# Scaling half of the query features by a ratio of softmax sums, in a four-layer kernel on one Trainium2 core

## The chip, the cores and the metric

The kernel runs on one core of a Trainium2 chip. The metric is the device time of one execution in microseconds (us); lower is better. A core has a matrix engine (PE, with weight loads listed apart as PEld), a vector engine (DVE), an activation engine (ACT), a general engine (POOL), and SP, which here only issues DMAs. Each engine works through its own stream of instructions in order, and they wait for one another through semaphores.

## The reference, cut to what matters

Two kinds of layer alternate: A, B, A, B. Each adds its result to `x` after a layer norm. Layer A goes through 64 segments of 32 tokens; the memory of a segment comes out of the segment before, so A is a chain. Layer B is linear attention; its features are softmaxes over the 20 features of a head:

```python
pq = einsum('bhsd,hdf->bhsf', q, w_phi);  pk = the same of k
phi_q = concatenate([softmax(pq), softmax(-pq)], axis=-1)
phi_k = concatenate([softmax(pk), softmax(-pk)], axis=-1)
kv = einsum('bhsf,bhsd->bhfd', phi_k, v)
z  = sum over s of phi_k
o  = einsum('bhqf,bhfd->bhqd', phi_q, kv) / (einsum('bhqf,bhf->bhq', phi_q, z) + 1e-06)
```

There are 2048 tokens, width 640, 32 heads of 20 features, two halves (called `sg` 0 and 1 in the kernel). A factor that is common to both halves of `phi_q` of one token and head appears above and below the line of the last quotient.

## The kernel before

**Layer A.** `A_pre` first computes what doesn't depend on the chain. `A_chain` then runs the 64 segments. One segment is, on PE, twelve projections of 20 matmuls with 32 weight columns each (`project`, L943, results `ps_qk` and `ps_v`), scores (`ps_s`), sums, attention (`ps_o`), four rounds of 48 output matmuls (`wo_round`, L1019, `ps_w`), and 14 matmuls into a spare bank (`keep_busy`, L1026, `ps_idle`). Its order is written out by hand. The weights of a segment stream in from HBM all the time, issued by SP. In the first segment of a chain `fill(FILL[li])` puts weight loads of one column each into PE's stream after the first projection; every segment has `SEG_FILL` = 1 more. They compute nothing.

**Layer B.** `layer_B` works on four groups of 512 tokens. Heads are packed six to a chunk of 120 partitions (`CH`), six chunks (`NC_`), the last of two heads; a feature array `phi` has a half, a chunk and a token index. In each group `keys_values` does keys and values; `queries` (L447) multiplies out the query features and ACT writes `exp(pq)` and `exp(-pq)` into both halves of `phi` (L450); `query_norms`, one group later, makes them softmaxes:
- 12 matmuls with the 0/1 matrix `osum` add up the features of each head and half in one bank, `ps_sq` (L457);
- `reciprocal_rows` makes the reciprocals as `exp(-log(sum))` on ACT, Ln L346, Exp L348 (bf16) and Exp L349 (fp32), and a DVE subtraction L350 leaves in the upper 64 partitions the remainder that bf16 lost;
- 12 matmuls with the 0/1 matrix `expd` spread the reciprocals over the features (`ps_e`, L464), and DVE multiplies each chunk of each half in place (L465).

After the last group `kvm` and `zm` are taken from PSUM (L511, L514). The tail then does, for each group, `denominators` (12 matmuls into `ps_den`, L522, and `reciprocal_rows` again), `attention` (L533, L536, L538, L539) and `output_rows` (L550, L552, and in the first B layer the next layer norm, whose centring is L244 on POOL). `query_norms` of the last group stands after `attention(0)`. `late_constants` builds `osum`, `zm` and `expd` during group 1 on POOL (L318, L324, L326, L329). `side_bank` is a pool of two PSUM banks that `ps_sq`, `ps_e` and `ps_den` share. Inside layer B the order of each engine's instructions is set by a planner, with the program's order as its input; the A layers are outside it.

Of the kernel before, what the change touches and what calls it, by code (L numbers as in the profile page):

```python
# [17 lines left out]
SLOTS = {"Q": 3, "K": 3, "V": 3}  # L18
LN_EPS = 1e-5

FILL = {0: 86, 2: 78}
SEG_FILL = 1

LATE = 64512
# [3 lines left out]
def ap3(ap, dims):  # L28
    return bass.AP(tensor=ap.tensor, offset=ap.offset, ap=[list(d) for d in dims])
# [86 lines left out]
class Kernel:  # L116
# [133 lines left out]
    def layer_B(self, x_dram, at_dram, xout_dram, xnext_dram, li, bp, post):  # L250


        nc, tc, KC, D = self.nc, self.tc, self.KC, self.Dm
        DH, H = self.DhB, self.HB
        HC = 6
        CH = DH * HC
        NC_ = -(-H // HC)
        sizes = [min(CH, D - CH * c) for c in range(NC_)]
# [5 lines left out]
        def take(nbytes):  # L264
            nonlocal at
            at += nbytes
            return at - nbytes

        f4 = NC_ * 512 * 2
        wo = self.view(take(NC_ * D * 2), NC_ * D * 2).rearrange("p (c m) -> p c m", m=D)  # L270
        osum, zm = [self.view(take(f4 // 2), f4 // 2).rearrange("p (s c m) -> p s c m", s=2, m=P) for _ in range(2)]
        expd = self.view(take(4 * NC_ * CH), 4 * NC_ * CH).rearrange("p (s c d) -> p s c d", s=2, d=DH)
        kvm = self.view(take(4 * NC_ * CH), 4 * NC_ * CH).rearrange("p (s c m) -> p s c m", s=2, m=CH)
        lgs, hls = self.views(take(4096), 2048, 2, F32), self.views(take(2048), 1024, 2)
        oTs = self.views(take(2 * f4), f4, 2)
# [6 lines left out]
        blk = self.view(take(32), 2 * HC)  # L282
# [10 lines left out]
        phi = self.view(ARENA - fb, fb).rearrange("p (s c t) -> p s c t", s=2, c=NC_)  # L293
        with tc.tile_pool(name=f"B{li}_kv", bufs=1, space=bass.MemoryType.PSUM, reuse_waits="tile") as kvp, \
                tc.tile_pool(name=f"B{li}_pt", bufs=2, space=bass.MemoryType.PSUM, reuse_waits="tile") as ptp, \
                tc.tile_pool(name=f"B{li}_ps", bufs=3, space=bass.MemoryType.PSUM, reuse_waits="tile") as pp:
            def bank(name="ps_b", dt=F32):
                return pp.tile([P, 512 if dt == F32 else 1024], dt, name=name, tag="bank")

            def side_bank(name):  # L300
                return ptp.tile([P, 512], F32, name=name, tag="side")

            nc.gpsimd.memset(wbd[:], 0.0)
            for i in range(HC):
# [10 lines left out]
            expc = expd[:, :, :, :].rearrange("p s (c h) d -> p s c (h d)", h=HC)  # L315

            def late_constants():
                nc.gpsimd.memset(osum[:], 0.0)  # L318
                nc.vector.memset(zm[:], 0.0)
                for sg in range(2):  # L320
                    for c in range(NC_):
                        nh = sizes[c] // DH
                        o = osum[:, sg, c, :].rearrange("p (u h) -> p u h", u=2)[:, :, 32 * sg + HC * c:32 * sg + HC * c + nh]
                        nc.gpsimd.tensor_copy(out=o, in_=bcast_mid(blk[:, 0:nh], 2))  # L324

                nc.gpsimd.memset(expd[:], 0.0)  # L326
                for sg in range(2):
                    for u in range(2):
                        nc.gpsimd.affine_select(out=expd[:, sg], in_=expd[:, sg], compare_op=ALU.not_equal, fill=1.0,  # L329
                                                base=-(32 * sg + 64 * u), pattern=[[-1, NC_ * HC], [0, DH]],  # L330
                                                channel_multiplier=1)
# [3 lines left out]
            eps6 = bp.tile([P, 1], F32, name="eps6")  # L335
            nc.vector.memset(eps6[:], 1e-6)
            kv_ps = [kvp.tile([P, 512], F32, name=f"kv{j}") for j in range(3)]

            def kv_out(sg, c):
                j = NC_ * sg + c  # L340
                return kv_ps[j // 4][0:sizes[c], 126 * (j % 4):126 * (j % 4) + 21 * (sizes[c] // DH)]

            def reciprocal_rows(ps, bias):

                lg = lgs.next()
                nc.scalar.activation(out=lg[:], in_=ps[:, :], func=ACT.Ln, bias=bias)  # L346
                hl = hls.next()
                nc.scalar.activation(out=hl[:], in_=lg[:], func=ACT.Exp, scale=-1.0)  # L348
                nc.scalar.activation(out=lg[64:P, :], in_=lg[64:P, :], func=ACT.Exp, scale=-1.0)  # L349
                nc.vector.tensor_tensor(out=hl[64:P, :], in0=lg[64:P, :], in1=hl[64:P, :], op=ALU.subtract)  # L350
                return hl

            def load_rows(g):
                for b in range(4 * g, 4 * g + 4):
# [96 lines left out]

            def query_norms(g):
                tk = slice(512 * g, 512 * g + 512)
                ps = side_bank("ps_sq")
                for i in range(2 * NC_):
                    sg, c = i // NC_, i % NC_
                    nc.tensor.matmul(ps[:, :], lhsT=osum[0:sizes[c], sg, c, :], rhs=phi[0:sizes[c], sg, c, tk],  # L457
                                     start=(i == 0), stop=(i == 2 * NC_ - 1))
                hl = reciprocal_rows(ps, 0.0)
                for i in range(2 * NC_):  # L460
                    sg, c = i // NC_, i % NC_
                    mc = sizes[c]
                    pe = side_bank("ps_e")
                    nc.tensor.matmul(pe[0:mc, :], lhsT=expc[:, sg, c, 0:mc], rhs=hl[:, :], start=True, stop=True)  # L464
                    nc.vector.tensor_tensor(out=phi[0:mc, sg, c, tk], in0=phi[0:mc, sg, c, tk], in1=pe[0:mc, :], op=ALU.mult)  # L465


            with tc.issue_after(self.last_load.ins):
# [38 lines left out]
            for sg in range(2):  # L507
                for c in range(NC_):
                    mc, nh = sizes[c], sizes[c] // DH
                    o = kv_out(sg, c).rearrange("p (h f) -> p h f", f=DH + 1)  # L510
                    nc.vector.tensor_tensor(out=kvm[0:mc, sg, c, 0:mc].rearrange("p (h f) -> p h f", f=DH), in0=o[:, :, 0:DH],  # L511
                                            in1=mask[0:mc, 0:nh, :], op=ALU.mult)
                    for u in range(2):
                        nc.vector.tensor_tensor(out=zm[0:mc, sg, c, 64 * u + HC * c:64 * u + HC * c + nh], in0=o[:, :, DH],  # L514
                                                in1=blk[0:mc, 0:nh], op=ALU.mult)

            def denominators(g):
                tk = slice(512 * g, 512 * g + 512)
                ps = side_bank("ps_den")
                for i in range(2 * NC_):  # L520
                    sg, c = i // NC_, i % NC_
                    nc.tensor.matmul(ps[:, :], lhsT=zm[0:sizes[c], sg, c, :], rhs=phi[0:sizes[c], sg, c, tk],  # L522
                                     start=(i == 0), stop=(i == 2 * NC_ - 1))
                return reciprocal_rows(ps, eps6[:])

            def attention(g, hl):
                tk = slice(512 * g, 512 * g + 512)
                oT = oTs.next().rearrange("p (c t) -> p c t", c=NC_)
                for c in range(NC_):
                    mc = sizes[c]  # L530
                    pn = bank("ps_num")
                    for sg in range(2):
                        nc.tensor.matmul(pn[0:mc, :], lhsT=kvm[0:mc, sg, c, 0:mc], rhs=phi[0:mc, sg, c, tk], start=(sg == 0),  # L533
                                         stop=(sg == 1))
                    pe = side_bank("ps_e")
                    nc.tensor.matmul(pe[0:mc, :], lhsT=expc[:, 0, c, 0:mc], rhs=hl[:, :], start=True, stop=True)  # L536
# [335 lines left out]
    def A_chain(self, xn_dram, at_dram, li, load_slot, piece, load_wo, late_wo, wo_mid, wo_end, low):  # L872
# [3 lines left out]
        with tc.tile_pool(name=f"A{li}_ch", reuse_waits="tile", bufs=1) as sp, \  # L876
# [196 lines left out]
            for s in range(NSEG):  # L1073
# [19 lines left out]
                if s == 0:  # L1093
                    fill(FILL[li])
                to_rows(q_or_k("K", 0), "K")
# [141 lines left out]
```

## Time and profile before

| what | value |
|---|---|
| median of 3 runs | 3733.62 us (3727.46 to 3739.32) |
| profiled execution | 3733.58 us, of which 3731.6 us are the span |
| PE, DVE, ACT, POOL busy | 95%, 63%, 55%, 45% of the span |
| first chain, first to last store of a segment | 1345.75 us |
| from there to the first store of the second chain (first B layer, second `A_pre`) | 501.3 us |
| second chain, first to last store | 1405.15 us |
| from there to the end (second B layer) | 272.5 us |

The stages are bounded by the stores of a segment's rows (`attn<-Vp`, 64 in each chain). The shares are averages over stages with different limits, so the table by stage says more than the busy shares of the whole. "Idle before" in a list of groups is the idle time of an engine just before the instructions of that group, and "issue" stands for time in which the engine waited for nothing that the profile names.

### The profile page before, as it was taken

How to read it: one execution, taken by the hardware profiler on the slowest of the kernel's cores; microseconds unless marked ns; L12 is line 12 of the kernel's file. 1: busy time of each engine (PE TensorE's matmuls, PEld its weight loads, DVE VectorE, ACT ScalarE, POOL GpSimd, SP SyncE). 2: the span in 40 equal slices, each digit the busy share in tenths (PEclk: the TensorE clock that was granted, in tenths of full speed). 3: DMA queues.
4: the chain of work that ended last, by engine and by line, in shares of the span. 5: the costliest groups of instructions: out<-in, count | busy, mean ns of one | idle time of the engine just before them, and what ended most of it. 6: DMA issues, size and time to landing. Idle time of an engine off the chain costs nothing.

```text
span 3731.6 us, 168901 instructions
## 1 busy us (share of the span) xinstructions
PE 3537.4 (95%) x71010; PEld 2312.5 (62%) x71318; DVE 2365.5 (63%) x6334; ACT 2038.1 (55%) x5225; POOL 1665.2 (45%) x4325
## 2 busy tenths in 40 slices
PE   9999999999999999989898999999999999999898
PEld 7766666666666666555376666666666666665553
DVE  6566666666666666466633666666666666666475
ACT  3356666666666656455423655556555555555363
POOL 3345555555555555330622444454444444544400
PEclk9999999999999999989899999999999999999999
DMA  9988788887888878812297778777777777877500
GB/s 304 336 296 288 277 286 282 286 293 278 291 280 288 295 267 296 299 59 81 95 290 235 273 265 281 279 264 273 274 272 279 263 270 279 283 272 276 171 1 29
DMA packets 531731, 933.33 MB, mean 250 GB/s; under 512 B 141066, under 2 KB 298394, under 8 KB 530970
## 3 DMA queue, kind: packets, MB, share of 16 engines
q1 hardware_dynamic: 428794, 818.87, 62.3%
q0 software_dynamic: 68512, 90.42, 7.9%
q10 hardware_dynamic: 33664, 13.24, 1.4%
q8 instruction: 557, 9.13, 1.0%
q14 instruction: 204, 1.67, 0.1%
HBM read 852.43 MB, written 73.73 MB: 248 GB/s over the span
## 4 chain that ended last, share of the span: by engine, by line
PE 38%; DVE 6%; ACT 4%; issue 4%; DMA 2%; PEld 2%; POOL 2%; SPq 0%; POOLq 0%; DVEq 0%; ACTq 0%
PE ps_qk L943 10%; PE ps_v L943 5%; PE ps_w L1019 5%; PE ps_o L993 3%; PE ps_s L985 2%; DVE hT L899 2%; PE ps_s L1051 2%; PE ps_pq L447 2%; PE ps_s L980 1%; PEld L834 1%; PE ps_pre L834 1%; PE ps_idle L1026 1%; PE ps_v L426 1%; DVE E L1058 1%; ACT raw L953 1%
## 5 line engine op out<-in xcount | busy, mean ns | idle before, releaser
L943 PEld LDWEIGHTS <-hT 128*32 128x32 bf16 x30720 | 745.0, 96 | 507.0 <-issue 90.4
L943 PE MATMUL ps_qk<-arena,hT 128*32 128x384 bf16 x20480 | 1004.5, 328 | 14.8 <-DMA arena<-in_A_Wq_dram 2.8
L953 ACT ACTIVATE raw<-ps_qk 128x384 bf16<-128x384 f32 x1024 | 503.0, 491 | 382.1 <-PE ps_s L1051 246.3
L943 PE MATMUL ps_v<-arena,hT 128*32 128x384 bf16 x10240 | 569.0, 330 | 43.7 <-issue 36.2
L926 POOL DMA_DIRECT2D Vp<-vb x512 | 259.6, 507 | 716.9 <-PE ps_o L993 473.1
L1019 PE MATMUL ps_w<-arena,OT 128*32 128x160 bf16 x24576 | 533.1, 235 | 15.8 <-DMA arena<-wo_rows 9.5
L1019 PEld LDWEIGHTS <-OT 128*32 128x32 bf16 x24576 | 434.3, 97 | 101.6 <-issue 25.1
L958 DVE STREAM_TRANSPOSE KT<-raw 128x384 bf16<-128x384 bf16 x512 | 296.2, 578 | 197.7 <-ACT raw L953 193.7
L961 DVE STREAM_TRANSPOSE QT<-raw 128x256 bf16<-128x256 bf16 x512 | 228.0, 445 | 238.4 <-ACT raw L953 196.0
L914 POOL DMA_DIRECT2D kqb<-kqb x512 | 292.3, 571 | 174.6 <-POOL KT L922 146.2
L974 DVE CAST Vp<-ps_v 64x384 bf16<-64x384 f32 x512 | 286.2, 559 | 118.7 <-ACT Vp L972 103.1
L972 ACT ACTIVATE Vp<-ps_v 64x384 bf16<-64x384 f32 x512 | 246.3, 481 | 175.5 <-PE ps_v L943 135.8
L999 DVE CAST OT<-ps_o 128x192 bf16<-128x192 f32 x512 | 183.3, 358 | 247.3 <-PE ps_o L993 228.3
L1012 POOL DMA_DIRECT2D otb<-otb x512 | 283.9, 554 | 111.3 <-DVE otb L1008 97.4
L1058 DVE TENSOR_TENSOR E<-E,ps_s 80x320 bf16<-80x320 bf16 x512 | 247.4, 483 | 73.4 <-ACT ps_s L1057 69.4
L1037 ACT ACTIVATE E<-ps_s 80x320 bf16<-80x320 f32 x512 | 221.9, 433 | 124.3 <-PE ps_s L985 95.4
L993 PEld LDWEIGHTS <-Vp 80*128 80x128 bf16 x4096 | 183.0, 99 | 157.1 <-issue 117.1
L998 ACT ACTIVATE OT<-ps_o 128x192 bf16<-128x192 f32 x512 | 167.9, 328 | 178.2 <-PE ps_o L993 176.9
L907 ACT ACTIVATE Vp<-ps_w 32x160 bf16<-32x160 f32 x512 | 150.7, 294 | 205.7 <-DVE wt L1162 132.7
L993 PE MATMUL ps_o<-E,Vp 80*128 80x80 bf16 x4096 | 234.7, 202 | 25.7 <-DVE E L1058 7.4
L985 PE MATMUL ps_s<-QT,KT 128*80 128x80 bf16 (+1 forms) x3072 | 233.4, 213 | 21.4 <-DVE KT L958 13.1
L919 POOL COPY QT<-kqb 128x64 bf16<-128x64 bf16 x512 | 126.5, 247 | 252.3 <-PE ps_s L985 244.1
(156 smaller groups left out, 5442.2 us busy)
## 6 DMA issues: line engine op xcount, KB each, us to landing
arena<-wo_rows SPq DMA_DIRECT2D x792, 320.0 KB, 6.7
arena<-in_A_Wq_dram SPq DMA_DIRECT2D x427, 384.0 KB, 4.5
arena<-in_A_Wv_dram SPq DMA_DIRECT2D x427, 384.0 KB, 6.5
arena<-in_A_Wk_dram SPq DMA_DIRECT2D x768, 192.0 KB, 5.2
kqb<-kqb POOLq DMA_DIRECT2D x512, 48.0 KB, 5.1
arena<-in_A_Wk_dram SPq DMA_DIRECT2D x43, 384.0 KB, 6.7
vb<-arena POOLq DMA_DIRECT2D x128, 112.0 KB, 5.8
Vp<-vb POOLq DMA_DIRECT2D x512, 28.0 KB, 4.9
```

What stands on the lines that cost most here:

```text
L914: nc.gpsimd.dma_start(out=kqb[:], in_=self.kqb_d[s, :, r, :])
L926: nc.gpsimd.dma_start(out=Vs[n % 2][64:80, :], in_=self.vb_d[s, r].rearrange("g t f -> (g t) f"))
L943: nc.tensor.matmul(o[32 * g:32 * g + 32, 0:384], lhsT=hT[:, b, :], rhs=rhs, start=(i == 0), stop=(i == KC - 1), tile_position=(0, 32 * g), ...
L953: nc.scalar.activation(out=raw[:], in_=ps[:, 0:384], func=ACT.Copy)
L958: nc.vector.transpose(out=KT[:, :, 0:64], in_=raw[:, :].rearrange("p (c j) -> p c j", j=64))
L972: nc.scalar.activation(out=o, in_=i, func=ACT.Copy)
L974: nc.vector.tensor_copy(out=o, in_=i)
L985: nc.tensor.matmul(S[0:80, c0:c0 + 80 * (q1 - q0)], lhsT=KT[:, 3 * x + i, :], rhs=QT[:, x, q0:q1, :], start=False, stop=(x == 1 and i == 2 ...
L993: nc.tensor.matmul(O[x][:, 80 * i:80 * i + 80], lhsT=Vs[n % 2][0:80, 448 * x + k:448 * x + k + 128], rhs=E[0:80, 160 * x + 80 * e:160 * x ...
L1012: nc.gpsimd.dma_start(out=self.otb_d[s, :, 96 * r:96 * r + 96], in_=otb[:, :, :].rearrange("p c t -> p (c t)"))
L1019: nc.tensor.matmul(W[32 * g:32 * g + 32, 0:160], lhsT=OT[:, c, q:q + 32], rhs=w[:, 640 * i + 160 * g:640 * i + 160 * g + 160], start=(firs ...
L1058: nc.vector.tensor_tensor(out=E[0:80, 0:320], in0=E[0:80, 0:320], in1=rc, op=ALU.mult)
```

## The change

A token's query features are no longer divided by the sums of both halves. The first half stays `exp(pq)`; the second half is multiplied by S+/S-, the ratio of the two sums, so that both halves carry the common factor S+. The 1e-06 in the denominator becomes 1e-06 added to `z` of the first half, which S+ multiplies as well. The sums of the halves come from two accumulations of 6 matmuls into two banks; the ratio is `exp(log S+ - log S-)`. Only 6 spreading matmuls and 6 multiplications a group remain. Rows go from 128 to 64 partitions in the sums and denominators, and the constants shrink to match. `FILL` of the second chain goes from 78 to 79.

```diff
-FILL = {0: 86, 2: 78}
+FILL = {0: 86, 2: 79}
...
-                for sg in range(2):
-                    for c in range(NC_):
...
+                for c in range(NC_):
+                    nh = sizes[c] // DH
+                    o = osum[:, c, :].rearrange("p (u h) -> p u h", u=2)[:, :, HC * c:HC * c + nh]
+                    nc.gpsimd.tensor_copy(out=o, in_=bcast_mid(blk[:, 0:nh], 2))
...
+                for u in range(2):
+                    nc.gpsimd.affine_select(out=expd[:], in_=expd[:], compare_op=ALU.not_equal, fill=1.0, base=-32 * u,
+                                            pattern=[[-1, NC_ * HC], [0, DH]], channel_multiplier=1)
...
-            def reciprocal_rows(ps, bias):
...
+            def split_exp(lg, scale):
+                hl = hls.next()
+                nc.scalar.activation(out=hl[0:64, :], in_=lg[0:64, :], func=ACT.Exp, scale=scale)
+                nc.scalar.activation(out=lg[32:64, :], in_=lg[32:64, :], func=ACT.Exp, scale=scale)
+                nc.vector.tensor_tensor(out=hl[32:64, :], in0=lg[32:64, :], in1=hl[32:64, :], op=ALU.subtract)
+                return hl[0:64, :]
+
+            def log_rows(ps):
                 lg = lgs.next()
+                nc.scalar.activation(out=lg[0:64, :], in_=ps[0:64, :], func=ACT.Ln)
+                return lg
...
             def query_norms(g):
                 tk = slice(512 * g, 512 * g + 512)
-                ps = side_bank("ps_sq")
-                for i in range(2 * NC_):
...
-                hl = reciprocal_rows(ps, 0.0)
-                for i in range(2 * NC_):
-                    sg, c = i // NC_, i % NC_
+                lg = []
+                for sg in (1, 0):
+                    ps = side_bank("ps_sq")
+                    for c in range(NC_):
+                        nc.tensor.matmul(ps[0:64, :], lhsT=osum[0:sizes[c], c, :], rhs=phi[0:sizes[c], sg, c, tk],
+                                         start=(c == 0), stop=(c == NC_ - 1))
+                    lg.append(log_rows(ps))
+                nc.vector.tensor_tensor(out=lg[0][0:64, :], in0=lg[1][0:64, :], in1=lg[0][0:64, :], op=ALU.subtract)
+                hl = split_exp(lg[0], 1.0)
+                for c in range(NC_):
                     mc = sizes[c]
                     pe = side_bank("ps_e")
-                    nc.tensor.matmul(pe[0:mc, :], lhsT=expc[:, sg, c, 0:mc], rhs=hl[:, :], start=True, stop=True)
-                    nc.vector.tensor_tensor(out=phi[0:mc, sg, c, tk], in0=phi[0:mc, sg, c, tk], in1=pe[0:mc, :], op=ALU.mult)
+                    nc.tensor.matmul(pe[0:mc, :], lhsT=expc[0:64, c, 0:mc], rhs=hl, start=True, stop=True)
+                    nc.vector.tensor_tensor(out=phi[0:mc, 1, c, tk], in0=phi[0:mc, 1, c, tk], in1=pe[0:mc, :], op=ALU.mult)
...
+                        z = zm[0:mc, sg, c, 32 * u + HC * c:32 * u + HC * c + nh]
+                        if sg == 0:
+                            nc.vector.scalar_tensor_tensor(out=z, in0=o[:, :, DH], scalar=1e-6, in1=blk[0:mc, 0:nh], op0=ALU.add,
+                                                           op1=ALU.mult)
+                        else:
+                            nc.vector.tensor_tensor(out=z, in0=o[:, :, DH], in1=blk[0:mc, 0:nh], op=ALU.mult)
...
-                return reciprocal_rows(ps, eps6[:])
+                return split_exp(log_rows(ps), -1.0)
```

More of the change, by code (lines that the diff above doesn't have):

```diff
@@ L270, in layer_B @@
         wo = self.view(take(NC_ * D * 2), NC_ * D * 2).rearrange("p (c m) -> p c m", m=D)
-        osum, zm = [self.view(take(f4 // 2), f4 // 2).rearrange("p (s c m) -> p s c m", s=2, m=P) for _ in range(2)]
-        expd = self.view(take(4 * NC_ * CH), 4 * NC_ * CH).rearrange("p (s c d) -> p s c d", s=2, d=DH)
+        osum = self.view(take(NC_ * P), NC_ * P).rearrange("p (c m) -> p c m", m=P // 2)
+        zm = self.view(take(2 * NC_ * P), 2 * NC_ * P).rearrange("p (s c m) -> p s c m", s=2, m=P // 2)
+        expd = self.view(take(2 * NC_ * CH), 2 * NC_ * CH).rearrange("p (c d) -> p c d", d=DH)
         kvm = self.view(take(4 * NC_ * CH), 4 * NC_ * CH).rearrange("p (s c m) -> p s c m", s=2, m=CH)
@@ L313, in layer_B @@
             nc.gpsimd.tensor_copy(out=mask[:], in_=bcast_last(blk[:], DH))
-            expc = expd[:, :, :, :].rearrange("p s (c h) d -> p s c (h d)", h=HC)
+            expc = expd[:, :, :].rearrange("p (c h) d -> p c (h d)", h=HC)
             def late_constants():
@@ L319, in late_constants @@
                 nc.vector.memset(zm[:], 0.0)
-                for sg in range(2):
-                    for c in range(NC_):
[L322 to L331, printed above, removed]
+                for c in range(NC_):
+                    nh = sizes[c] // DH
+                    o = osum[:, c, :].rearrange("p (u h) -> p u h", u=2)[:, :, HC * c:HC * c + nh]
+                    nc.gpsimd.tensor_copy(out=o, in_=bcast_mid(blk[:, 0:nh], 2))
+                nc.gpsimd.memset(expd[:], 0.0)
+                for u in range(2):
+                    nc.gpsimd.affine_select(out=expd[:], in_=expd[:], compare_op=ALU.not_equal, fill=1.0, base=-32 * u,
+                                            pattern=[[-1, NC_ * HC], [0, DH]], channel_multiplier=1)
                 for c in range(NC_):
                     nc.sync.dma_start(out=wo[0:sizes[c], c, :], in_=self.B_wo[CH * c:CH * c + sizes[c], :])
-            eps6 = bp.tile([P, 1], F32, name="eps6")
-            nc.vector.memset(eps6[:], 1e-6)
             kv_ps = [kvp.tile([P, 512], F32, name=f"kv{j}") for j in range(3)]
@@ L341, in kv_out @@
                 return kv_ps[j // 4][0:sizes[c], 126 * (j % 4):126 * (j % 4) + 21 * (sizes[c] // DH)]
-            def reciprocal_rows(ps, bias):
-                lg = lgs.next()
[L346 to L351, printed above, removed]
+            def split_exp(lg, scale):
[5 more added lines that the diff above has]
+            def log_rows(ps):
+                lg = lgs.next()
+                nc.scalar.activation(out=lg[0:64, :], in_=ps[0:64, :], func=ACT.Ln)
+                return lg
             def load_rows(g):
@@ L453, in query_norms @@
                 tk = slice(512 * g, 512 * g + 512)
-                ps = side_bank("ps_sq")
-                for i in range(2 * NC_):
-                    sg, c = i // NC_, i % NC_
-                    nc.tensor.matmul(ps[:, :], lhsT=osum[0:sizes[c], sg, c, :], rhs=phi[0:sizes[c], sg, c, tk],
-                                     start=(i == 0), stop=(i == 2 * NC_ - 1))
-                hl = reciprocal_rows(ps, 0.0)
-                for i in range(2 * NC_):
-                    sg, c = i // NC_, i % NC_
+                lg = []
[8 more added lines that the diff above has]
+                for c in range(NC_):
                     mc = sizes[c]
                     pe = side_bank("ps_e")
-                    nc.tensor.matmul(pe[0:mc, :], lhsT=expc[:, sg, c, 0:mc], rhs=hl[:, :], start=True, stop=True)
-                    nc.vector.tensor_tensor(out=phi[0:mc, sg, c, tk], in0=phi[0:mc, sg, c, tk], in1=pe[0:mc, :], op=ALU.mult)
+                    nc.tensor.matmul(pe[0:mc, :], lhsT=expc[0:64, c, 0:mc], rhs=hl, start=True, stop=True)
+                    nc.vector.tensor_tensor(out=phi[0:mc, 1, c, tk], in0=phi[0:mc, 1, c, tk], in1=pe[0:mc, :], op=ALU.mult)
             with tc.issue_after(self.last_load.ins):
@@ L513, in layer_B @@
                     for u in range(2):
-                        nc.vector.tensor_tensor(out=zm[0:mc, sg, c, 64 * u + HC * c:64 * u + HC * c + nh], in0=o[:, :, DH],
-                                                in1=blk[0:mc, 0:nh], op=ALU.mult)
+                        z = zm[0:mc, sg, c, 32 * u + HC * c:32 * u + HC * c + nh]
[4 more added lines that the diff above has]
+                            nc.vector.tensor_tensor(out=z, in0=o[:, :, DH], in1=blk[0:mc, 0:nh], op=ALU.mult)
             def denominators(g):
@@ L521, in denominators @@
                     sg, c = i // NC_, i % NC_
-                    nc.tensor.matmul(ps[:, :], lhsT=zm[0:sizes[c], sg, c, :], rhs=phi[0:sizes[c], sg, c, tk],
+                    nc.tensor.matmul(ps[0:64, :], lhsT=zm[0:sizes[c], sg, c, :], rhs=phi[0:sizes[c], sg, c, tk],
                                      start=(i == 0), stop=(i == 2 * NC_ - 1))
-                return reciprocal_rows(ps, eps6[:])
+                return split_exp(log_rows(ps), -1.0)
             def attention(g, hl):
@@ L535, in attention @@
                     pe = side_bank("ps_e")
-                    nc.tensor.matmul(pe[0:mc, :], lhsT=expc[:, 0, c, 0:mc], rhs=hl[:, :], start=True, stop=True)
+                    nc.tensor.matmul(pe[0:mc, :], lhsT=expc[0:64, c, 0:mc], rhs=hl, start=True, stop=True)
                     rx = rxs.next()
```

## The prediction

> **What bounds the kernel now.** I read the page for the shares, then the table by stage, then the list of groups of each stage. The page says that PE is busy 95% of the span, and the granted clock is full nearly everywhere: PE's stream is the limit in most stages. But the table by stage, with the two chains as stages, shows that the same 64 segments do not take the same time twice:
>
> ```profile
> core 0: us, PE busy (x) PEld busy (x) DVE busy (x) ACT busy (x) POOL busy (x), PEclk, DMA share, GB/s
> 206.89:1552.64 1345.75, 1309.21 (x32104) 863.99 (x32161) 921.26 (x2578) 830.51 (x2207) 692.65 (x1890) 1.00 0.82 286
> 2053.95:3459.10 1405.15, 1339.17 (x32102) 870.10 (x32159) 921.09 (x2578) 826.87 (x2207) 691.94 (x1890) 1.00 0.79 274
> ```
>
> Equal work, equal clock, and 59.4 us more in the second chain. The lists of PE's groups in these two windows say where; first chain first, each time the matmul and then the weight load:
>
> ```profile
> L943 PE MATMUL ps_v<-arena,hT 128*32 128x384 bf16 x5040 | 262.8, 329 | 0.0
> L943 PEld LDWEIGHTS <-hT 128*32 128x32 bf16 x15076 | 360.6, 96 | 207.4 <-DVE hT L1163 14.8 <-issue 1.3
> ...
> L943 PE MATMUL ps_v<-arena,hT 128*32 128x384 bf16 x5040 | 294.9, 329 | 38.1 <-issue 36.2
> L943 PEld LDWEIGHTS <-hT 128*32 128x32 bf16 x15076 | 366.7, 96 | 279.6 <-issue 77.0 <-DVE hT L1163 15.3
> ```
>
> The idle time before `ps_v` goes from 0.0 to 38.1 us and no semaphore ends it ("issue"). One instance, in the timeline of PE:
>
> ```profile
> 2445.97 0.67 PE L943 MATMUL ps_v<-arena,hT 128*32 128x384 bf16 x10
> 2447.27 0.34 PE L943 MATMUL ps_v<-arena,hT 128*32 128x384 bf16 x2 [0.64 <-issue]
> ```
>
> Ten matmuls of a projection run, then PE stands still 0.64 us in the middle of it, with weights and inputs there.
>
> [...] the page's queue line
>
> ```profile
> q8 instruction: 557, 9.13, 1.0%
> ```
>
> (packets, MB, share) is 9.13 MB / 557 = 16.4 KB each, and 557 x 256 = 142,592 against 71,010 + 71,318 PE and PEld instructions. [...] Counted in order of start, the records of PE, PEld and PE's own waits come to 1024 a segment (510 matmuls, 511 weight loads, 3 waits): **exactly four blocks**, so the edges of blocks fall on the same places in every segment of a chain. In the second chain all 64 unexplained stops over 0.25 us stand at one residue of that count modulo 256, at places 495, 751 and 1007 after a segment's last `ps_idle`; together they are 37.0 us. At place 751 the stopped matmul starts typically 1.4 us after an instruction packet has ended. In the first chain the 11 such stops (4.2 us) all stand at place 798, inside `wo_round`.
>
> 798 - 751 = 47. The count between like points of the two chains gives it again: 71,463 records, plus 8 matmuls missing in the first B layer (L1193 has 184 of 192 beside 192 weight loads): 71,471 = 279 x 256 + 47. So the chains differ in **phase** by 47 instructions. Projections are PE's fast stretches (40 instructions in 0.8 us)[...]. Matmul by matmul, the median segment of the second chain falls behind by 0.41 us at place 495 and by 0.70 us at place 751, and wins back 0.19 us where the first chain has its own waits: 0.92 us, times 64 is 59 us.
>
> **The change part by part.**
>
> (1) *PE's count ahead of the second chain.* `query_norms` loses 6 of 12 `ps_e` matmuls a group, each with its weight load; the sums stay 12. In the first B layer that is 4 x 6 x 2 = 48 instructions fewer, and `FILL` adds one weight load: 48 - 1 = 47 fewer. If the waits in PE's stream stay as many (the trace has 3 in the first B layer and 6 in the second `A_pre`), the second chain comes to stand exactly in the first chain's phase. I price it at the first chain's measured time: 1345.75 - 1405.15 = **-59.4 us**. Two or four waits more or fewer would move the edges by as much; the first chain's third edge already stops 11 times in 64, so I allow +10 us for that, and -4 us were those stops to go. The added load itself is under 0.1 us. The first chain comes before any edit: zero.
>
> (2) *Layer B, three groups of `query_norms` amid keys and queries* (1628 to 1754 us in the first B layer). PE is busy 18 to 19.8 us of every 20 there. The rows, of the window 1640 to 1850 us:
>
> ```profile
> L465 DVE TENSOR_TENSOR arena<-arena,ps_e 120x512 bf16<-120x512 bf16 x40 | 26.1, 676 | 5.1 <-PE ps_e L464 4.9
> L464 PE MATMUL ps_e<-arena 128*120 128x512 bf16 x40 | 14.6, 381 | 2.3 <-DVE arena L350 1.3 <-DVE arena L465 0.8
> L350 DVE TENSOR_TENSOR arena<-arena 64x512 bf16<-64x512 f32 x8 | 5.5, 690 | 10.8 <-ACT arena L349 10.7
> L348 ACT ACTIVATE arena<-arena 128x512 bf16<-128x512 f32 x8 | 5.0, 630 | 0.2
> L349 ACT ACTIVATE arena<-arena 64x512 f32<-64x512 f32 x8 | 5.0, 626 | 0.2
> L346 ACT ACTIVATE arena<-ps_sq 128x512 f32<-128x512 f32 x4 | 2.4, 602 | 1.2 <-PE ps_sq L457 1.2
> ```
>
> [...]the 12 `ps_sq` in 3.08 us give (3.08 - 0.38)/11 = 0.245. I take 0.24. Removed in three groups: 18 x 0.24 = 4.3 us of PE and about half of its 2.3 us of waits; 18 x 0.68 = 12.2 us of DVE, which mostly lies beside PE. Added: one Ln a group (0.60 us of ACT) and one fp32 subtraction (0.69 us of DVE, as L350). Going from 128 rows to 64 saves nothing: L348 and L349 show 630 and 626 ns. Behind the added Ln on ACT stand the exponentials L414 and L450, for which PE waited 2.3 and 2.0 us in this stage: up to +1.8. The subtraction waits for both Lns, and behind it on DVE stand L430 and L417; DVE's relief covers that. Sum: -4 us (-7 to -1).
>
> (3) *`late_constants`.* POOL's four rows in its timeline:
>
> ```profile
> 1611.42 1.38 POOL L318 MEMSET arena<- 128x1536 bf16 x1
> 1612.86 1.62 POOL L324 COPY arena<-arena 128x12 bf16<-128x12 bf16 x12
> 1614.42 1.30 POOL L326 MEMSET arena<- 128x1440 bf16 x1
> 1615.80 4.03 POOL L329 TENSOR_SCALAR_AFFINE_SELECT arena<-arena 128x720 bf16<-128x720 bf16 x4
> ```
>
> A quarter, a half, a half and a half of this stay: 0.35 + 0.81 + 0.65 + 2.0 = 3.8 instead of 8.3 us, so POOL reaches the additions L361 queued behind it 4.5 us sooner. PE is busy 35.8 of 40 us there and fills the time with other matmuls: -1 us (-4 to 0). The DVE memset of `zm` halves, SP's loads of `wo` are the same, both beside PE: zero.
>
> (4) *The tail.* `query_norms` of the last group: 6 x 0.24 = -1.4 us of PE. The chain of waits passes through the DVE run
>
> ```profile
> 1781.14 4.27 DVE arena L465 x7
> ```
>
> while `output_rows`' L552 waits behind it on DVE, and POOL behind that; half of that run goes, about -2.5. The logs and the extra subtraction make the reciprocals later by 0.69 us; `ps_wo` matmuls cover it, at worst +0.7. `scalar_tensor_tensor` for 12 of the 24 L514 (0.15 us each) is not in the trace; at best the same, at worst double: 0 to +1.8, I take 0.5. POOL's L244, 16 of 1.9 us in the first B layer, then paces the rows and gives some back. `denominators` keeps its count: zero. Sum: -2 us (-5 to +2).
>
> A B layer: -4 - 1 - 2 = -7 us (-16 to +1); two of them **-14** (-25 to 0, the planner's other order included). The sum is made against the profiled execution, 3733.58 us (span 3731.6 and 2.0 around it), which is the median of the runs, 3733.62, within 0.04: 3733.6 - 59.4 - 14 = **3660**.
>
> **The rivals.**
> - *B's gain alone.* The stalls have another cause, or waits change by so many that the edges fall as badly: 3733.6 - 14 = 3720 (3709 to 3734). For it: I infer the edges, the profile names no cause. Against: one residue for all 64 stops, another 47 away for the 11 of the first chain. Chance 9%.
> - *The new phase is worse; slower.* One more edge a segment falls late in a projection and waits as long as that at place 751, 0.70 us: 64 x 0.70 = +45, less 14: 3765. It decides once the stops exceed today's by 14/64 = 0.22 us a segment. Against: the arithmetic lands on a phase whose time is seen. Chance 3%.
> - *Phase right, B gives nothing:* each extra ACT step lands before an exponential that PE awaits: 3733.6 - 59.4 = 3674, within the range.
>
> **How the numbers follow.** Phase regained 88%, rival one 9%, rival two 3%. A difference of 0.3% (11 us) is about what can be told from no change. Phase regained is all faster; of rival one some 5 are faster, 4 the same. Faster 0.93, same 0.04, slower 0.03. The likeliest case runs from 3733.6 - 63 - 25 = 3645 to 3733.6 - 49 - 0 = 3684; I give 3642 to 3688, which leaves out the rivals and little more.
>
> **What would show it.** The second chain as a stage takes 1346 +- 10 us, `ps_v` there shows idle near 0 before it, and unexplained stops stand only at place 798. The rows of L464 and L465 have half the counts with unchanged means, an Ln row of 64x512 has double the count, POOL's constants take about 4 us. The two B stages are 501 and 272 us now and should be some 7 shorter each. A second chain near 1405 us would overturn the main term; a B stage longer by more than 2 us would overturn parts 2 to 4.

## The result, and the profile after

The changed kernel takes **3686.77 us** (median; 3680.76 to 3696.94) where the kernel before, beside it, takes 3730.54 us: a ratio of 0.9884 with a 95% interval of 0.9849 to 0.9919. It is faster, by 44 us and not by the 73 us that were forecast; the time lies at the upper end of the stated range (3642 to 3688).

The table by stage of the changed kernel (columns as in the prediction: window, length, busy time with counts of PE, PEld, DVE, ACT and POOL, granted clock, DMA share, GB/s), in the order first chain, second chain, first B layer with the second `A_pre`, second B layer:

```profile
207.14:1557.06 1349.92, 1310.82 (x32103) 864.80 (x32159) 920.82 (x2577) 830.53 (x2207) 690.10 (x1890) 1.00 0.83 285
2062.23:3404.99 1342.76, 1309.17 (x32103) 863.00 (x32159) 920.98 (x2577) 830.49 (x2207) 689.39 (x1891) 1.00 0.83 287
1557.06:2062.23 505.17, 469.03 (x3448) 293.70 (x3530) 241.47 (x530) 200.46 (x424) 150.44 (x273) 0.91 0.51 160
3404.99:3678.80 273.81, 246.40 (x1472) 131.59 (x1470) 146.61 (x315) 117.19 (x238) 48.97 (x91) 0.95 0.19 60
```

The two B rows of the kernel before, for comparison:

```profile
1552.64:2053.95 501.31, 454.41 (x3463) 293.83 (x3550) 253.46 (x550) 198.12 (x420) 153.98 (x280) 0.94 0.51 161
3459.10:3731.60 272.50, 241.35 (x1491) 135.34 (x1496) 159.16 (x335) 115.01 (x234) 52.11 (x99) 0.96 0.19 59
```

The second chain fell from 1405.15 to 1342.76 us. The B stages did not become shorter: 501.31 to 505.17 and 272.50 to 273.81. The first chain, which no edit precedes, took 1349.92 instead of 1345.75 (its stops at place 798 are 18 with 9.6 us, where the kernel before had 11 with 4.2), and the stretch ahead of it 0.25 us more. In sum -62.4 + 3.9 + 1.3 + 4.2 + 0.25 = -52.8 us, the difference of the two spans (3731.6 and 3678.8). Look at PE in the first B stage: 20 DVE instructions fewer and fewer matmuls, and yet PE is busy 14.6 us *longer*, at a lower clock.

The groups of the second chain, matmul and weight load of a projection, after:

```profile
L948 PE MATMUL ps_v<-arena,hT 128*32 128x384 bf16 x5040 | 262.4, 328 | 0.0
L948 PEld LDWEIGHTS <-hT 128*32 128x32 bf16 x15076 | 360.2, 96 | 206.8 <-DVE hT L1168 14.2 <-issue 0.9
```

The 38.1 us of idle time before `ps_v` are gone. The 10 stops over 0.25 us that are left in this chain (4.4 us) all stand at place 798, where the first chain has its own. The count of PE's records between like points of the two chains is now 71,424 = 279 x 256: phase difference zero.

POOL's constants, in its timeline (start, duration, line, operation):

```profile
1614.94 0.42 POOL L319 MEMSET arena<- 128x384 bf16 x1
1615.43 0.85 POOL L324 COPY arena<-arena 128x12 bf16<-128x12 bf16 x6
1616.21 0.70 POOL L326 MEMSET arena<- 128x720 bf16 x1
1616.99 2.15 POOL L328 TENSOR_SCALAR_AFFINE_SELECT arena<-arena 128x720 bf16<-128x720 bf16 x2
```

They take 4.1 us instead of 8.3. The groups of `query_norms` in layer B (busy time, mean ns of one, then the idle time before them), after:

```profile
L466 DVE TENSOR_TENSOR arena<-arena,ps_e 120x512 bf16<-120x512 bf16 x20 | 13.2, 666 | 0.9 <-PE ps_e L465 0.7
L465 PE MATMUL ps_e<-arena 64*120 64x512 bf16 x20 | 7.3, 404 | 0.7 <-DVE arena L344 0.7
L457 PE MATMUL ps_sq<-arena 120*64 120x512 bf16 x40 | 13.8, 451 | 0.0
L349 ACT ACTIVATE arena<-ps_sq 64x512 f32<-64x512 f32 x8 | 4.7, 589 | 3.5 <-PE ps_sq L457 3.5
```

and the sums in the kernel before:

```profile
L457 PE MATMUL ps_sq<-arena 120*128 120x512 bf16 x40 | 11.3, 380 | 0.1
```

The spread has half the count, as it should. The mean of the 40 sums rose from 380 ns with 128 weight columns to 451 ns with **64**, over the same 512 tokens, and that of the spread from the 381 ns that the prediction shows to 404 ns with 64 rows. This mean mixes two things: the sums of the first three groups take 390 to 394 ns on average, those of the last group 634 ns. A narrow sum by itself is hardly slower here (390 to 394 ns against 380); something around it changed.

PE's timeline in the tail shows what, and it is two things. The kernel before, where `denominators` and `attention` take turns (start, duration):

```profile
1755.18 0.38 PE L522 MATMUL ps_den<-arena 120*128 120x512 bf16 x1
1755.40 0.38 PE L533 MATMUL ps_num<-arena 120*120 120x512 bf16 x1
1755.62 0.38 PE L522 MATMUL ps_den<-arena 120*128 120x512 bf16 x1
1755.83 0.38 PE L533 MATMUL ps_num<-arena 120*120 120x512 bf16 x1
```

and the same place after:

```profile
1755.88 0.43 PE L538 MATMUL ps_num<-arena 120*120 120x512 bf16 x1
1756.24 0.40 PE L527 MATMUL ps_den<-arena 120*64 120x512 bf16 x1
1756.57 0.43 PE L538 MATMUL ps_num<-arena 120*120 120x512 bf16 x1
1756.93 0.40 PE L527 MATMUL ps_den<-arena 120*64 120x512 bf16 x1
```

From start to start it was 0.22 us; now it is 0.33 to 0.36 us, with nothing waited for. What differs is that each matmul has another width of weights than the one before it. The second thing is the clock. The 12 `ps_sq` of the last group, before and then after:

```profile
1770.70 3.08 PE L457 MATMUL ps_sq<-arena 120*128 120x512 bf16 x12
...
1772.53 5.74 PE L457 MATMUL ps_sq<-arena 120*64 120x512 bf16 x12
```

In the second B layer of the changed kernel, in the full clock, the same 12 narrow sums take no longer than wide ones:

```profile
3605.94 3.12 PE L457 MATMUL ps_sq<-arena 120*64 120x512 bf16 x12
```

The tail of the first B layer, first `ps_den` to last `ps_wo`, by the table by stage, before and then after:

```profile
1752.90:1850.40 97.50, 81.39 (x336) 33.00 (x334) 58.93 (x158) 39.07 (x80) 45.56 (x70) 0.86 0.39 132
...
1753.60:1857.10 103.50, 94.93 (x331) 34.47 (x329) 53.47 (x131) 39.69 (x82) 45.73 (x70) 0.74 0.37 124
```

The granted clock falls from 0.86 to 0.74: the share withheld times the length goes from 13.7 to 26.9 us. So the question for the experiments is double: is it the phase that saved the 62 us, and what in layer B ate the 14?

### The profile page after: what moved, and what is told of

It is laid out like the page before. It is cut to its first block, busy times and chain, and to the rows that moved or that the text cites. A ratio compares the mean times of both kernels' runs of the same rounds, so it can differ in the third digit from the quotient of the medians.

```text
span 3678.8 us, 168780 instructions
## 1 busy us (share of the span) xinstructions
PE 3527.4 (96%) x70978; PEld 2301.1 (63%) x71271; DVE 2339.3 (64%) x6292; ACT 2044.9 (56%) x5233; POOL 1653.2 (45%) x4309
## 4 chain that ended last, share of the span: by engine, by line
PE 37%; DMA 6%; DVE 4%; ACT 3%; issue 3%; PEld 2%; POOL 1%; SPq 0%; POOLq 0%; ACTq 0%; DVEq 0%
PE ps_qk L948 10%; PE ps_w L1024 4%; PE ps_v L948 4%; PE ps_o L998 2%; PE ps_s L990 2%; DMA arena<-wo_rows 2%; PE ps_pq L446 1%; PE ps_s L1056 1%; PEld L839 1%; DVE hT L904 1%; PE ps_s L985 1%; DMA kqb<-arena 1%; PE ps_idle L1031 1%; DMA arena<-in_A_Wv_dram 1%; PE ps_pk L410 1%
## 5 line engine op out<-in xcount | busy, mean ns | idle before, releaser
L1024 PE MATMUL ps_w<-arena,OT 128*32 128x160 bf16 x24576 | 540.9, 234 | 27.5 <-issue 14.9
L948 PE MATMUL ps_v<-arena,hT 128*32 128x384 bf16 x10240 | 537.4, 330 | 5.6 <-DMA arena<-in_A_Wv_dram 5.5
L990 PEld LDWEIGHTS <-KT 128*80 128x80 bf16 x3072 | 195.0, 119 | 70.7 <-issue 60.9
```

Source lines behind the costliest of these rows:

```text
L948: nc.tensor.matmul(o[32 * g:32 * g + 32, 0:384], lhsT=hT[:, b, :], rhs=rhs, start=(i == 0), stop=(i == KC - 1), tile_position=(0, 32 * g), ...
L990: nc.tensor.matmul(S[0:80, c0:c0 + 80 * (q1 - q0)], lhsT=KT[:, 3 * x + i, :], rhs=QT[:, x, q0:q1, :], start=False, stop=(x == 1 and i == 2 ...
L1024: nc.tensor.matmul(W[32 * g:32 * g + 32, 0:160], lhsT=OT[:, c, q:q + 32], rhs=w[:, 640 * i + 160 * g:640 * i + 160 * g + 160], start=(firs ...
```

## The experiments

Seven kernels. "B stages" is the sum of the two B rows of the table by stage, "switches" the number of matmuls in both B layers whose operand goes from 40 or 64 rows or columns to 120 or 128, or back, against the matmul before it (counted from the trace; a plain count of all neighbours from the first matmul to the last `ps_wo` of each layer gives 427, 558, 501, 470, 414 and 40 in the order of the table), "tail" and "clock" the first B layer's tail as above. A step from 120 to 128 is no switch, since at 512 columns in the full clock the next matmul starts 0.215 to 0.220 us after it where nothing is waited for, nor is one from 40 to 64, with 0.216 us in the changed kernel; both are as short as between matmuls of one shape (0.216). The times of stages come from one profiled execution of each kernel.

| kernel | median us | ratio to before (95%) | second chain | B stages | switches | tail | clock |
|---|---|---|---|---|---|---|---|
| before | 3730.54 | 1 | 1405.2 | 773.8 | 423 | 97.5 | 0.86 |
| changed | 3686.77 | 0.9884 (0.9849 to 0.9919) | 1342.8 | 779.0 | 548 | 103.5 | 0.74 |
| before_fill31 | 3677.54 | 0.9858 (0.9835 to 0.9881) | 1351.7 | 770.5 | as before | 95.5 | 0.89 |
| after_fill126 | 3737.44 | 1.0013 (1.0003 to 1.0023) | 1399.5 | 782.4 | as changed | 109.3 | 0.67 |
| wide_sums | 3682.79 | 0.987 (0.9851 to 0.9888) | 1350.0 | 769.7 | 493 | 101.7 | 0.73 |
| wide_rows | 3671.15 | 0.9835 (0.9812 to 0.9858) | 1352.8 | 755.8 | 463 | 90.8 | 0.91 |
| wide_sums_rows | 3657.73 | 0.9801 (0.9782 to 0.9819) | 1354.0 | 740.1 | 402 | 87.9 | 0.92 |
| one_shape | 3643.94 | 0.9764 (0.9738 to 0.979) | 1353.5 | 726.2 | 39 | 83.2 | 0.88 |
| after_fill0_70 | 3700.44 | 0.9924 (0.9895 to 0.9952) | 1355.9 | 772.2 | as changed | 102.0 | 0.75 |

The rows with the same layer B give the noise of a stage: the B stages of the changed layer B come to 779.0, 782.4 and 772.2 us in three profiles, of the old one to 773.8 and 770.5; the tails (102 to 109 us against 95.5 to 97.5) and their clocks (0.67 to 0.75 against 0.86 to 0.89) stay apart. The second chain with `FILL` 79, or 31 in the old kernel, varies from 1342.8 to 1354.0 us.

**before_fill31: the phase alone.** The kernel before, with 47 padding loads fewer ahead of the second chain and nothing else:

```diff
-FILL = {0: 86, 2: 78}
+FILL = {0: 86, 2: 31}
```

> The kernel before with FILL of the second chain 31 instead of 78: 47 weight loads fewer ahead of it, layer B untouched. Phase theory (the edges of instruction blocks decide the second chain's time): second chain, first to last store, 1345 +- 5 us instead of 1405, unexplained stops only at place 798 of a segment, both B stages as before (501 and 272 us), in all about -60 us, near 3671. Rival (the change in layer B, its memory layout or its timing, is what freed the second chain): 1405 us as before, in all 3730.

Measured: 3677.54 us, 56 us less than the kernel before, and 9 us less than the changed kernel (their intervals overlap). Its second chain, and the projections in it:

```profile
2051.28:3402.94 1351.66, 1313.09 (x32103) 865.29 (x32159) 921.05 (x2578) 832.19 (x2207) 691.76 (x1891) 0.99 0.82 285
...
L943 PE MATMUL ps_v<-arena,hT 128*32 128x384 bf16 x5040 | 262.2, 328 | 0.0
```

The unexplained stops (15, together 6.9 us) stand at place 798 alone. No arithmetic was touched, and the 38.1 us before `ps_v` are gone: the phase is the cause of the first term. The changed kernel's second chain, 1342.76 us, is the shortest of all in this phase; the five other kernels with the same phase show 1350.0 to 1354.0 us, so the phase gives 51 to 62 us.

**after_fill126: the change without its phase.** The changed kernel with 47 padding loads more, which puts the second chain back where it was:

```diff
-FILL = {0: 86, 2: 79}
+FILL = {0: 86, 2: 126}
```

> The changed kernel with FILL 126 instead of 79: 47 weight loads more, which is the phase that the second chain had before. Phase theory: second chain back at about 1405 us with stops at places 495 and 751, in all +60 us on the changed kernel, near 3747, so slower than the kernel before by what layer B lost (about +5 to +15). Rival (layer B freed the chain): the time of the changed kernel, 3687.

Measured: 3737.44 us, no gain at all. The stops are back at 751 (41), 495 (13) and 1007 (1), together 34.8 us:

```profile
2068.29:3467.76 1399.47, 1337.38 (x32103) 868.65 (x32159) 921.02 (x2577) 827.81 (x2207) 691.84 (x1891) 1.00 0.79 275
...
L948 PE MATMUL ps_v<-arena,hT 128*32 128x384 bf16 x5040 | 293.8, 329 | 36.6 <-issue 34.5
```

Read together, the two kernels part the change: at equal phase the kernel with the new layer B takes 9 us more (3686.77 against 3677.54, not clear of the noise) or some 4 us more (3737.44 against 3733.46 beside it, an interval of 1 to 9 us that leaves out zero), where the prediction had it save 14.

**wide_sums: sums of 128 columns again.** `osum` and `zm` get 64 columns of zeros, so that the sums and denominators have 128 columns as before; the arithmetic that is read stays the same.

```diff
-        osum = self.view(take(NC_ * P), NC_ * P).rearrange("p (c m) -> p c m", m=P // 2)
+        osum = self.view(take(2 * NC_ * P), 2 * NC_ * P).rearrange("p (c m) -> p c m", m=P)
...
-                        nc.tensor.matmul(ps[0:64, :], lhsT=osum[0:sizes[c], c, :], rhs=phi[0:sizes[c], sg, c, tk],
+                        nc.tensor.matmul(ps[:, :], lhsT=osum[0:sizes[c], c, :], rhs=phi[0:sizes[c], sg, c, tk],
```

(and the same for `zm` and `ps_den`)

> The changed kernel with osum and zm padded with zero columns to 128, so that ps_sq and ps_den have 128 output rows again; the order of instructions on PE, DVE, ACT stays that of the changed kernel. Clock theory (matmuls with 64 weight columns leave PE's clock at half speed for longer in the tail of layer B: 61 us of halved clock in the first B layer's tail against 31 before, 25 against 12 in the second): halved clock about as before, ps_sq of the last group in about 3 us instead of 5.7, the first B stage some 5 us and the second some 4 us shorter, in all -8 to -14. Rival (the planner's order and the longer way to the ratio thin PE out, and the clock only follows): no change within 3 us.

Measured: 3682.79 us, only 4 us below the changed kernel, which the noise can make; B stages 9.3 us shorter, about the spread of the same layer B in three profiles. The tail's clock did not recover:

```profile
1752.50:1854.20 101.70, 94.05 (x330) 33.42 (x329) 53.64 (x131) 39.77 (x82) 46.23 (x70) 0.73 0.37 128
```

So the narrow *columns* are at most the smaller part, and the idea that they alone draw the clock down is wrong.

**wide_sums_rows: the spread reads 128 rows as well.** In addition the rows 64 to 127 of the reciprocals are set to zero once, and the spread reads all 128 rows; `expd`'s lower rows meet zeros.

```diff
+                for h in hls.rr.items:
+                    nc.vector.memset(h[64:P, :], 0.0)
...
-                return hl[0:64, :]
+                return hl[:, :]
...
-                    nc.tensor.matmul(pe[0:mc, :], lhsT=expc[0:64, c, 0:mc], rhs=hl, start=True, stop=True)
+                    nc.tensor.matmul(pe[0:mc, :], lhsT=expc[:, c, 0:mc], rhs=hl, start=True, stop=True)
```

> As wide_sums, and the spreading matmuls ps_e read 128 rows again (rows 64 to 127 of the reciprocals are zeros, set once). Clock theory: the halved clock shrinks a little further, 0 to -4 us against wide_sums. Rival: the same as wide_sums[...].

Measured: 3657.73 us, 29 us below the changed kernel and 25 below wide_sums, far more than expected. PE's matmuls come in the same order as in wide_sums and in the changed kernel, so the planner's other order, which these share, isn't what made layer B slower; B stages fall from 769.7 to 740.1 us, and the tail's clock is back:

```profile
1746.70:1834.60 87.90, 74.19 (x331) 30.91 (x330) 52.45 (x131) 39.56 (x81) 45.75 (x70) 0.92 0.43 147
```

This miss led to the count of switches. Over all matmuls of the B layers with 512 columns in the same clock, a matmul of the same shape as its forerunner starts 0.216 us after it, one after a switch 0.31 to 0.33 us; at 320 columns it is 0.136 and 0.232, at 126 columns 0.059 and 0.146. In the halved clock the pair at 512 columns is 0.427 and 0.56. The difference is 0.09 to 0.11 us at all three lengths and 0.13 in the halved clock, so it goes here by the switch and not by the column. What PE does in that time was not shown. The kernel before had 423 switches, the changed one 548.

**wide_rows: the 128 rows alone.** Only the second of the two edits, on the changed kernel.

> The changed kernel with ps_e reading 128 rows (rows 64 to 127 zeros) and the sums left at 64 columns. Shape-switch theory: a matmul starts 0.10 us later (0.31 against 0.216 us at 512 columns, full clock; 0.14 at half clock)[...]; both B layers together have 423 such switches before, 548 in the changed kernel, 493 in wide_sums, 402 in wide_sums_rows. The ps_e matmuls stand between others, so they make most of the added switches: about 460 here, 8 to 18 us under the changed kernel, near 3672. Rival (the halved clock follows the width of the sums alone): no better than wide_sums, 3683.

Measured: 3671.15 us, -15.6 against the changed kernel, with 463 switches. Rows alone bring the clock back, with the sums still at 64 columns:

```profile
1756.10:1846.90 90.80, 76.87 (x330) 31.79 (x328) 52.38 (x131) 39.51 (x82) 45.60 (x69) 0.91 0.43 142
```

Together with wide_sums this makes the rows the larger part (B stages -23.2 us) and the columns the smaller (-15.7 on top of the rows; the -9.3 alone is within the noise). The clock goes with the rows in every execution, not only in the profiled one: its mean over the whole kernel is 0.977 to 0.984 in all 30 executions of the four kernels whose spread reads 64 rows, and 0.985 to 0.988 in all 12 of wide_rows, wide_sums_rows and one_shape.

The traces also show what the rows do. In the traces of the kernel before and of the changed one the granted clock is 1.00 or 0.50, and from one change to the next it is each time a whole multiple of 3.41 us (from 1 to 391 times that). Here are three stretches of that length of the changed kernel's first tail, by the table by stage:

```profile
1758.71:1762.12 3.41, 1.01 (x4) 0.51 (x4) 1.03 (x2) 2.20 (x4) 0.00 (x0) 1.00 1.01 383
1768.95:1772.36 3.41, 3.41 (x8) 0.96 (x7) 0.00 (x0) 0.00 (x0) 0.00 (x0) 0.50 0.65 247
1775.78:1779.19 3.41, 3.41 (x10) 1.23 (x9) 0.26 (x1) 0.88 (x2) 0.00 (x0) 0.50 0.01 2
```

In the first PE mostly waits, and the next stretch is halved. In the second PE is busy throughout, and the next one is still halved. The third is followed by the full clock. What tells them apart is the *row share*: the time in which PE streams columns (estimated from 0.216 us for 512 columns, 0.427 in the halved clock), each matmul counted by its rows out of 128, as a share of the stretch. It is 0.09, 0.67 and 0.79. Over the B layers of all nine profiles, 69 of 73 stretches in the full clock with a row share below 0.38 are followed by a halved one, and none of 1170 with 0.40 or more. Once the clock is halved, none of 86 stretches below 0.70 is followed by the full clock, and 65 of 67 from 0.76 on are (7 of 26 between). It is the same where PE streams for at least 85% of the stretch: 0 of 23, and 58 of 59. The columns don't show: all 10 stretches from 0.76 on in which the same share by columns is under 0.6 bring the clock back. So the clock fell where PE waited, about as often before as after (5 and 6 falls in both tails together), and stayed down for longer where the spread read 64 rows: 9 halved stretches in the tails before, 21 in the changed kernel, 20 in wide_sums, 6 in wide_rows.

**one_shape: no switches left.** wide_sums_rows, and the sixth chunk of two heads (40 rows) padded to 120 with zeros in `phi`, `kvm`, `wo`, `oT` and the keys, so that nearly all matmuls of layer B have one shape.

```diff
-                        nc.tensor.matmul(ps[0:mc, :], lhsT=wqkv[:, k, CH * c:CH * c + mc], rhs=xnT[:, k, :],
+                        nc.tensor.matmul(ps[0:CH, :], lhsT=wqkv[:, k, CH * c:CH * c + CH], rhs=xnT[:, k, :],
...
+                nc.vector.memset(phi[:, :, NC_ - 1, :], 0.0)
...
-                            nc.tensor.matmul(ps[:, 0:W2], lhsT=oT[0:sizes[c], c, q:q + P],
-                                             rhs=wo[0:sizes[c], c, W2 * u:W2 * u + W2], start=(c == 0), stop=(c == NC_ - 1))
+                            nc.tensor.matmul(ps[:, 0:W2], lhsT=oT[0:CH, c, q:q + P],
+                                             rhs=wo[0:CH, c, W2 * u:W2 * u + W2], start=(c == 0), stop=(c == NC_ - 1))
```

> As wide_sums_rows, and the sixth chunk of layer B, with 40 rows or columns, is padded with zeros to 120 in every matmul of the groups and the tail[...]. The number of matmuls stays. Shape-switch theory: 402 switches fall to under 80, 300 x 0.10 = 30 us less, less up to 4 us for the zeros that have to be written: 22 to 36 us under wide_sums_rows, near 3630. Rival (what wide_sums_rows won came from the clock alone, and it is back where it was before the change): within 5 us of wide_sums_rows, 3658.

Measured: 3643.94 us (3636.62 to 3649.74), the fastest version, 43 us below the changed kernel; but only 14 below wide_sums_rows, where 22 to 36 were expected. The second B stage gains 12.1 us, the first 1.8. In the first, the zeros have to be written (`phi`'s memset alone is 1.8 us of DVE) and the keys start 2 to 6 us later; and in the tail PE no longer sets the pace. Its waits there, the longest (total us, times, longest), and the row of the next layer norm on POOL:

```profile
PE ps_num L549 <- DVE arena L568: 5.6, 5, 1.9
...
L244 POOL TENSOR_SCALAR arena<-arena,ln_mvr 128x640 bf16<-128x640 bf16 x15 | 28.2, 1879 | 1.5
```

PE waits for DVE's row output, and 15 x 1.88 us of POOL stand beside a tail of 83 us. The 363 switches fewer than in wide_sums_rows gained 13.9 us in the B stages, 0.04 us each: one saved where PE waits anyway gained little.

**after_fill0_70: the stops moved off place 798.** The changed kernel with 16 loads fewer ahead of both chains, so that the places 256 apart, one of which is where both chains still stop, fall 16 places later.

```diff
-FILL = {0: 86, 2: 79}
+FILL = {0: 70, 2: 79}
```

> The changed kernel with FILL of the first chain 70 instead of 86: the edges of instruction blocks fall 16 instructions later in both chains, at places 46, 302, 558 and 814 of a segment. Phase theory[...]: the third edge is reached 0.17 us later, so the stops at 798 (10 to 20 of more than 0.25 us in each chain) become fewer and shorter at 814: 3 to 10 us less in all, 3677 to 3684. Rival[...]: as many stops at 814, 3687 within 4 us.

Measured: 3700.44 us, 14 us slower than the changed kernel. The stops followed to place 814, some 12 of them in each chain; they are about as many, and each chain became longer (1357.96 and 1355.91 us, where the kernels at the other phase show 1343 to 1360). The median segment ends 0.12 us (first chain) and 0.25 us (second) later than in the changed kernel, lost near place 1000, in the last `wo_round`. What is lost there is not settled, and with executions of 3696 to 3709 us against 3681 to 3697 the difference is little more than the noise; moving them off place 798 gained nothing.

## Why the prediction was right or wrong

- **Part (1), phase: right.** Predicted -59.4, measured -62.4 us, with the signs named: a count of 47, stops at place 798 alone, `ps_v` without idle time. before_fill31 and after_fill126 show it from both sides. That the size was met so closely is partly luck: the five other kernels at this phase gain 51 to 55 us, and the total lies only just inside the range.
- **Parts (2) and (3), three groups and the constants: about right.** From the start of the stage to the first `ps_den`, the end of keys and queries, the first B layer became 3.7 us shorter and the second 4.3; -5 was predicted. POOL's constants took 4.1 us for the 3.8 predicted; the rows of Ln (600 ns before, 591 after) and the bf16 Exp (629 and 630) kept their durations, and the fp32 subtraction, priced at 690 ns by L350, took 682.
- **Part (4), the tail: the step that failed.** Predicted -2 us, at worst +2. From the first `ps_den` to the last `ps_wo` it became longer: 97.5 to 103.5 us in the first B layer, and by 5.6 us in the second. Two terms were put at nothing. The first is the price of the new shapes on PE. "Going from 128 rows to 64 saves nothing" was read off ACT and holds there (626 to 630 ns in both kernels); on PE the sums, denominators and spreads that remain were left at their old cost. They are 64 columns or 64 rows among matmuls of 128: over both B layers, 125 switches more at 0.10 us are 12.5 us, against 48 removed matmuls x 0.216 = 10.4 us; some 28 of the switches lie in each tail. The second term is the clock, which the prediction called full nearly everywhere, though it stood at 0.86 in this tail already: with 64 rows it stayed halved for longer (16 stretches of 3.41 us in the first tail, 8 before), and 13 us more are withheld in the first tail, 7 in the second.
- **The two terms don't simply add.** Removal, switches and the clock of the first tail would give some 15 us more than before, where the B stages show +5.2: part of the slower PE time lies where PE waits in any case.
- **The sum over layer B.** The prediction said that a B stage longer by more than 2 us would overturn parts (2) to (4). The first one is longer by 3.9 us, so their sum is overturned, although (2) and (3) held. Its range was also too narrow by its own working: two layers of -16 to +1 are -32 to +2, and -25 to 0 was written.
- **The rivals.** "Phase right, B gives nothing" (3674) was nearest. But its reason, an Ln ahead of an awaited exponential on ACT, isn't what happened: first parts (2) and (3) gained, then PE lost it again in the tail.
- **What stays open.** That 64-row operands go along with the low clock is shown: wide_sums keeps them and stays at 0.73, wide_rows takes them away and comes to 0.91. That the row share is what counts, and not the switches, rests on a count in finished traces, as no run changes the one and keeps the other (among halved stretches with two switches and PE streaming for 85% or more, 0 of 20 below 0.72 came back, and 24 of 28 from there on). What stops PE was not shown. That it has to do with the blocks, the packets of the instruction queue, is an inference from the places, 256 apart, from 142,328 PE and PEld instructions to 557 packets, 255.5 each, and from the 1.4 us after the end of a packet; no run changes the packets. The first chain's +4.2 us has no edit behind it: with the same stream that chain took 1345.60 us in before_fill31 and 1348.34 us in after_fill126, and up to 1359.97 us in one_shape, a spread that the forecast's range had to carry.

## What to carry to other kernels

Going from 128 to 64 rows or columns wasn't free on PE in this kernel, so where an operand shrinks, count how often consecutive matmuls go from 64 or fewer rows or columns to 120 or more and back (0.10 us each here), look at the granted clock where PE also waits (0.74 in this tail with 64 rows, 0.91 with 128), and try padding with zeros, rows first; here that made the same arithmetic 29 us faster. Where a long hand-ordered stream repeats in a fixed number of instructions (1024 records a segment here), look for stops at fixed places of it: here a few padding instructions ahead of the stream (47, worth 56 us) moved them, and an edit that took away 48 instructions called for another number. When an edit carries both an arithmetic change and a new padding, measure each by itself: here the padding alone did at least as well as the two together.

## What the runs showed of the hardware

- A switch between consecutive matmuls, from 40 or 64 rows or columns to 120 or 128 or back, cost 0.09 to 0.11 us at 126, 320 and 512 columns in the full clock, 0.13 at 512 columns in the halved one.
- 12 sums of 64 columns took 5.74 us where 12 of 128 had taken 3.08, and all of that is the halved clock: in the full clock they took 3.12. The halved clock was granted in whole multiples of 3.41 us. By rows, counted over the B layers of nine profiles: of the halved stretches with a row share below 0.70 none of 86 was followed by the full clock, also none of the 23 in which PE streamed for 85% or more; of those from 0.76 on 65 of 67 were. The granted clock is 0.74 over a tail in which PE is busy 92% of the time (94.93 of 103.5 us).
- The stops moved with the stream, place for place: 47 padding loads moved them by 47, 16 by 16. The stops of the second chain before, 37.0 us at places 495, 751 and 1007, came with one phase; with the other, 4.4 us at place 798 stood in their stead.
